# Attention with memory and a two-layer MoE on one core: the keys' and queries' high part, and the memory matrix's low part, move to GpSimd

## The chip, the cores and the metric

One core of a Trainium2 chip runs the kernel. The metric is the device time of one execution in microseconds. The core has a tensor engine (PE, whose weight loads are PEld), VectorE (DVE), ScalarE (ACT), GpSimd (POOL), and SyncE (SP), on whose queue nearly all DMAs of this kernel are issued.

## The reference

Four batches with eight heads of 576 positions and 64 features go through causal attention plus a read of a memory matrix; the result of all heads is one row of 512 features per position and goes through two dense layers with a gate between.

```python
def _attn_ref(q, k, v, M_prev, z_prev, beta):          # q, k, v: (4, 8, 576, 64)
    scores = scale * np.matmul(q, k.transpose(0, 1, 3, 2))
    scores = np.where(causal, -1000000000.0, scores)
    a = np.exp(scores - scores.max(-1, keepdims=True))
    a /= a.sum(-1, keepdims=True) + 1e-09
    local = np.matmul(a, v)
    q_p = phi(q)                                        # x > 0 ? x + 1 : exp(x)
    mem_out = (q_p @ M_prev) / (q_p @ z_prev + 1e-06)   # per head
    g = 1.0 / (1.0 + np.exp(-beta))[None, :, None, None]
    return g * mem_out + (1 - g) * local

def _moe_ref(x, w_in, w_out):                           # x: (2304, 512)
    h = x @ w_in                                        # w_in: (512, 2048)
    g = h * (1.0 / (1.0 + np.exp(-1.702 * h)))
    return g @ w_out
```

## The kernel before, in words

Matrix products run on PE in a rounded 32-bit type (F32R). To keep precision an operand is split into a high part, which is the operand rounded to F32R, and a low part, the operand less its high part; a product is then made of high times high, low times high and high times low.

Two heads form a pair, so there are 16 pairs: batch b = 0 to 3, pair c = 0 to 3 in it. For every pair `load_kq` and `load_vq` (L343 to L365) load keys and queries into `kqr` (128 partitions, 576 + 640 columns), values into `vr`, the memory matrices into `mr`, queries by rows into `qr` and the normaliser into `zb`. `plan_prep` then prepares them: `split_hi` (L375) makes `hi`, the high part of `kqr`, 1216 columns wide; `split_lo_k` and `split_lo_q` make the low parts `lok` (576 columns) and `loq` (640) on POOL; `stack_hi` and `stack_lo` copy the three by DMA into the operand `W`; `vhi` and `vlo` split the values into `vs`; `msplit` (L418) makes `ms`, the memory matrix times the head's gate `gt`, in a high and a low part; `qmin`, `qexp`, `qphi` (L438) make `qp`, phi of the queries, which is then divided by its norm. Pairs of batch 0 go another way for `ms` (`mplain`) and compute fewer columns, since part of that batch is done at the start; the other 12 pairs use `msplit`. `plan_attend` makes the scores `ps` on PE, their mask and maximum on DVE (L499), the exponentials `a` on ACT (L505), their scaling on POOL (L508), the transposes `pt` on PE, their split into two `e` on ACT and DVE, the sums `po` over `vs` and `ms` on PE, and `xf` from `po` on DVE. The last 64 columns of the pair's positions (`at`, `tail`) go a like way. `xstore` (L654) writes `xf` of the pair to the tensor `xd` in HBM.

Once a batch's four pairs are stored, `plan_x` loads its chunks (of 256 and 320 columns for batch 0, of 288 for the others) back as `xl` and splits them into `xh` and `xl`, ACT and POOL. `first_moe` then has filler for PE: 16 blocks of 12 matmuls `pm` per chunk. Each block's result goes as `hk` to a tensor `gd` in HBM. The second layer (`acc`) runs after all attention.

A plan of slots puts the instructions into one program order: an entry of the plan has a slot and a priority, pair p starts at slot `K0[p]`, and a block of filler goes into each slot while there is any. The tile framework then reorders the instructions of every engine by a simulated schedule of its own; so an edit in one place changes the order in many. Each engine works its own list strictly in order, and so does SP's queue. `kqr`, `vr`, `mr`, `qr`, `zb`, `hi`, `lok` and `loq` have one buffer each, `W`, `vs` and `ms` have two: the next pair's load or write waits for the last reader of the one before.

`copy(engine, out, in, scale)` and `sub(engine, out, a, b)` are helpers (L97 and L112), with "A" for ACT, "P" for POOL and "V" for DVE; in the profile they stand as L100 (copy on ACT) and L110 (two-input operations).

Of the kernel before, what the change touches and what calls it, by code (L numbers as in the profile page):

```python
# [12 lines left out]
ALU = mybir.AluOpType  # L13
AX = mybir.AxisListType

B, H, S, D = 4, 8, 576, 64
# [6 lines left out]
SQ = 640  # L23
# [6 lines left out]
def f32(ap):  # L30
    return ap.bitcast(F32)
# [3 lines left out]
def tile_attention_memory_moe(ctx, tc, kq, vq, mem, zz, beta, w_in, w_out, out):  # L35
    nc = tc.nc
# [60 lines left out]
    def copy(eng, dst, src, scale=None):  # L97
        if eng == "A":
            kw = {} if scale is None else {"scale": scale}
            nc.scalar.activation(out=dst, in_=src, func=AF.Copy, **kw)  # L100
        elif eng == "V":
            if scale is None:
                nc.vector.tensor_copy(dst, src)
            else:
                nc.vector.tensor_scalar(out=dst, in0=src, scalar1=scale, scalar2=None, op0=ALU.mult)
        else:
            nc.gpsimd.tensor_copy(dst, src)

    def tt(eng, dst, a, b, op):
        (nc.vector if eng == "V" else nc.gpsimd).tensor_tensor(out=dst, in0=a, in1=b, op=op)  # L110

    def sub(eng, dst, src, hi):  # L112
        tt(eng, dst, src, f32(hi), ALU.subtract)
# [7 lines left out]
        out=mask[:, 384:512], in_=mask[:, 384:512], compare_op=ALU.is_ge, fill=NEG,  # L121
# [4 lines left out]
    for r in range(2):  # L126
        v = maskt[64 * r:64 * r + 64, CH - 64:CH]
        nc.gpsimd.affine_select(
            out=v, in_=v, compare_op=ALU.is_ge, fill=NEG, base=0, pattern=[[-1, 64]], channel_multiplier=1)
# [5 lines left out]
    gt = cst.tile([128, NP], F32, name="gt")  # L135
# [200 lines left out]
    raws = {}  # L336
# [30 lines left out]
    def plan_prep(p):  # L367
        b, c = pairs[p]
        s0 = K0[p] - 8
        P = prep[p] = {}  # L370
        rest = b < MB
        T0 = 2 if rest else 0
        qo = 256 if rest else 0

        def split_hi():  # L375
            kqr = raws[p]["kq"]
            P["hi"] = att.tile([128, S + SQ], F32R, name="hi")
            copy("A", P["hi"][:, :S + SQ - qo], kqr[:, :S + SQ - qo])

        def split_lo_k():  # L380
            P["lok"] = att.tile([128, S], F32R, name="lok")
# [35 lines left out]

        def msplit():  # L418
            P["ms"] = att.tile([128, 2, 2, D], F32R, name="ms", bufs=2)
            copy("A", P["ms"][:, :, 0], raws[p]["m"], gt[:, c:c + 1])  # L420
            nc.vector.scalar_tensor_tensor(
                out=P["ms"][:, :, 1], in0=raws[p]["m"], scalar=gt[:, c:c + 1], in1=f32(P["ms"][:, :, 0]),
                op0=ALU.mult, op1=ALU.subtract)

        qm = qmt[:, T0:, :, :D]

# [35 lines left out]
        def qev():  # L462
# [6 lines left out]
            for pt, a, n in ((P["pt"][0][:, qo:], qo, 512 - qo), (P["pt"][1], 512, 64)):  # L469
                copy("A", qh[:, a:a + n], pt[:, :n])  # L470
                sub("V", ql[:, a:a + n], pt[:, :n], qh[:, a:a + n])

        at(s0 + 1, 50, split_hi)
        at(s0 + 3, 50, split_lo_k)
        at(s0 + 3, 51, split_lo_q)
        at(s0 + 3, 52, stack_hi)
        at(s0 + 4, 52, stack_lo)
        if rest:
            at(s0 + 7, 51, mplain)
        else:  # L480
            at(s0 + 6, 55, vhi)
            at(s0 + 7, 50, vlo)
            at(s0 + 7, 51, msplit)
# [429 lines left out]
```

## Time and profile before

| | |
|---|---|
| time, median of 3 runs (lowest, highest) | 684.53 us (683.67, 687.51) |
| the profiled execution's own time | 687.52 us |
| its span in the trace | 685.6 us |
| busy PE / DVE / ACT / POOL | 629.7 / 435.1 / 396.4 / 263.7 us |

The span runs from the first to the last instruction of the trace. A row of the trace gives an instruction's start in the span and how long it took, then engine, line, operation and its tiles, output first. In brackets stands how long its engine was idle before it and what ended that wait. Matmuls are pipelined, so the times of neighbours overlap.

### The profile page before, as it was taken

How to read it: one execution, taken by the hardware profiler on the slowest of the kernel's cores; microseconds unless marked ns; L12 is line 12 of the kernel's file. 1: busy time of each engine (PE TensorE's matmuls, PEld its weight loads, DVE VectorE, ACT ScalarE, POOL GpSimd, SP SyncE). 2: the span in 40 equal slices, each digit the busy share in tenths (PEclk: the TensorE clock that was granted, in tenths of full speed). 3: DMA queues.
4: the chain of work that ended last, by engine and by line, in shares of the span. 5: the costliest groups of instructions: out<-in, count | busy, mean ns of one | idle time of the engine just before them, and what ended most of it. 6: DMA issues, size and time to landing. Idle time of an engine off the chain costs nothing.

```text
span 685.6 us, 12438 instructions
## 1 busy us (share of the span) xinstructions
PE 629.7 (92%) x3984; PEld 572.3 (83%) x3984; DVE 435.1 (63%) x1112; ACT 396.4 (58%) x960; POOL 263.7 (38%) x303
## 2 busy tenths in 40 slices
PE   4578898799987799999899997999999999999997
PEld 3468686689986699999899997999888888888897
DVE  4987765776758776677657634816865555555453
ACT  5676546787757775777576533614555445454453
POOL 3647545976636793566475202502400000000000
PEclk8699999999999999999999999999999999999999
DMA  8859758888557765766772128936444335344231
GB/s 252 270 158 262 217 139 239 231 211 222 150 156 206 206 186 168 216 164 181 236 206 71 44 79 292 323 115 222 152 123 142 109 102 154 94 126 133 68 125 55
DMA packets 71425, 116.70 MB, mean 170 GB/s; under 512 B 8768, under 2 KB 41024, under 8 KB 71360
## 3 DMA queue, kind: packets, MB, share of 16 engines
q1 hardware_dynamic: 71360, 115.91, 57.8%
q8 instruction: 32, 0.52, 0.3%
q14 instruction: 33, 0.27, 0.1%
HBM read 63.97 MB, written 27.79 MB: 134 GB/s over the span
## 4 chain that ended last, share of the span: by engine, by line
PE 73%; DMA 10%; DVE 7%; ACT 5%; issue 3%; SPq 1%; POOL 1%; ACTq 0%; DVEq 0%; POOLq 0%
PE acc L91 29%; PE pm L91 24%; PE po L91 9%; PE pt L95 6%; PE ps L91 5%; DMA gd<-hk 2%; DMA qr<-in_vq_dram 2%; DMA xl<-xd 2%; DMA xd<-xf 1%; DVE ps L499 1%; DMA fq<-in_vq_dram 1%; DVE ws L180 1%; DVE wr L182 1%; DVE ws L179 1%; DMA mr<-in_mem_dram 1%
## 5 line engine op out<-in xcount | busy, mean ns | idle before, releaser
L91 PE MATMUL pm<-xh,wi 128*128 128x288 f32 (+2 forms) x1024 | 221.3, 305 | 12.3 <-ACT hk L100 6.0
L91 PEld LDWEIGHTS pm<-xh,wi 128*128 128x128 f32 x1024 | 168.0, 192 | 15.9 <-ACT hk L100 6.9
L91 PE MATMUL acc<-gh,wo 128*128 128x512 f32 (+1 forms) x640 | 179.2, 368 | 0.0
L91 PE MATMUL pm<-xl,wi 128*128 128x288 f32 (+2 forms) x512 | 153.6, 301 | 0.1
L91 PEld LDWEIGHTS acc<-gh,wo 128*128 128x128 f32 x640 | 115.1, 189 | 20.1
L91 PE MATMUL acc<-gl,wo 128*128 128x512 f32 (+1 forms) x320 | 115.1, 368 | 0.0
L91 PEld LDWEIGHTS pm<-xl,wi 128*128 128x128 f32 x512 | 98.1, 192 | 0.7 <-POOL xl L110 0.3
L508 POOL TENSOR_SCALAR a<-a,sm,g 128x512 f32<-128x512 f32 (+3 forms) x112 | 71.9, 654 | 64.3 <-DVE sm L547 37.1
L499 DVE CUSTOM_DVE_ANT_0 ps<-ps,mask 128x256 f32<-128x256 f32 (+4 forms) x144 | 69.3, 495 | 20.7 <-PE ps L91 15.5
L813 DVE SCALAR_TENSOR_TENSOR gt<-gt,graw 128x512 f32<-128x512 f32 (+1 forms) x80 | 52.3, 654 | 45.5 <-ACT gt L812 45.0
L91 PE MATMUL po<-e,vs 128*128 128x320 f32 (+3 forms) x416 | 76.3, 308 | 4.5 <-ACT e L100 3.7
L505 ACT ACTIVATE a<-ps,nm 128x512 f32<-128x512 f32 (+3 forms) x112 | 60.2, 540 | 31.9 <-DVE nm L499 26.8
L812 ACT ACTIVATE gt<-graw 128x512 f32<-128x512 f32 (+1 forms) x80 | 47.0, 589 | 54.6 <-DVE gl L110 54.6
L110 DVE TENSOR_TENSOR gl<-gt,gh 128x512 fp32r<-128x512 f32 (+1 forms) x80 | 53.2, 665 | 37.2 <-ACT gh L100 34.1
L110 DVE TENSOR_TENSOR e<-pt,e 128x320 fp32r<-128x320 f32 (+1 forms) x120 | 56.4, 486 | 30.9 <-ACT e L100 30.3
L100 ACT ACTIVATE e<-pt 128x320 fp32r<-128x320 f32 (+4 forms) x136 | 55.7, 435 | 28.0 <-PE pt L95 15.0
L91 PEld LDWEIGHTS po<-e,vs 128*128 128x128 f32 x416 | 64.1, 192 | 9.2 <-ACT e L100 4.3
L100 ACT ACTIVATE gh<-gt 128x512 fp32r<-128x512 f32 (+1 forms) x80 | 47.0, 588 | 42.2 <-PE acc L91 39.6
L91 PEld LDWEIGHTS acc<-gl,wo 128*128 128x128 f32 x320 | 59.4, 189 | 9.9
L91 PE MATMUL ps<-W 128*128 128x512 f32 (+3 forms) x224 | 58.6, 347 | 4.6 <-DVE e L110 2.8
L95 PE MATMUL pt<-ident,a 128*128 128x128 f32 x296 | 57.5, 276 | 0.4 <-ACT a L505 0.4
L100 ACT ACTIVATE hk<-pm 128x288 f32<-128x288 f32 (+2 forms) x64 | 26.2, 409 | 52.5 <-PE pm L91 40.4
(132 smaller groups left out, 962.9 us busy)
## 6 DMA issues: line engine op xcount, KB each, us to landing
graw<-gd SPq DMA_DIRECT2D x64, 256.0 KB, 2.7
gd<-hk SPq DMA_DIRECT2D x96, 144.0 KB, 2.5
wraw<-in_w_in_dram SPq DMA_DIRECT2D x16, 512.0 KB, 4.3
wraw<-in_w_out_dram SPq DMA_DIRECT2D x16, 512.0 KB, 4.6
kqr<-in_kq_dram SPq DMA_DIRECT2D x12, 608.0 KB, 5.3
W<-hi SPq DMA_DIRECT2D x24, 272.0 KB, 3.6
W<-loq SPq DMA_DIRECT2D x48, 128.0 KB, 3.7
W<-lok SPq DMA_DIRECT2D x32, 144.0 KB, 3.3
```

Of the source, the lines that this page charges most:

```text
L91: nc.tensor.matmul(out, l, r, start=start, stop=stop)
L95: nc.tensor.transpose(out, in_, idn)
L100: nc.scalar.activation(out=dst, in_=src, func=AF.Copy, **kw)
L110: (nc.vector if eng == "V" else nc.gpsimd).tensor_tensor(out=dst, in0=a, in1=b, op=op)
L179: nc.vector.tensor_scalar(out=si, in0=si, scalar1=3, scalar2=None, op0=ALU.logical_shift_left)
L180: nc.vector.scalar_tensor_tensor(out=si, in0=raw[:, :, 1], scalar=-2 ** 31, in1=si, op0=ALU.bitwise_and, op1=ALU.bitwise_or)
L182: nc.vector.scalar_tensor_tensor(out=box["r"].bitcast(I32), in0=raw[:, :, 0], scalar=29, in1=si, op0=ALU.logical_shift_right, op1=ALU.bitw ...
L499: nc.vector.tensor_tensor_reduce(out=ps, in0=ps, in1=mk, op0=ALU.add, op1=ALU.min, scale=-0.125, scalar=1e38 if j == 0 else nm[:, j - 1:j] ...
L505: nc.scalar.activation(out=a, in_=ps, func=AF.Exp, scale=-1.0, bias=nm, accum_out=sm)
L508: (nc.vector if eng == "V" else nc.gpsimd).tensor_scalar(out=a, in0=a, scalar1=r, scalar2=gcol, op0=ALU.mult, op1=ALU.mult)
L812: nc.scalar.activation(out=t[:, :n], in_=raw[:, :n], func=AF.Tanh, scale=0.851)
L813: nc.vector.scalar_tensor_tensor(out=t[:, :n], in0=t[:, :n], scalar=1.0, in1=raw[:, :n], op0=ALU.add, op1=ALU.mult)
```

## The change

For pairs of batches 1 to 3, `split_hi`'s copy is made by POOL instead of ACT. For the same pairs `msplit` has another form: ACT first scales `mr` in its own place, then ACT copies it to the high part, and POOL subtracts for the low part; before, ACT scaled into the high part, and one DVE instruction (L421) scaled again and subtracted.

```diff
         def split_hi():
             kqr = raws[p]["kq"]
             P["hi"] = att.tile([128, S + SQ], F32R, name="hi")
-            copy("A", P["hi"][:, :S + SQ - qo], kqr[:, :S + SQ - qo])
+            copy("P" if b else "A", P["hi"][:, :S + SQ - qo], kqr[:, :S + SQ - qo])
...
         def msplit():
             P["ms"] = att.tile([128, 2, 2, D], F32R, name="ms", bufs=2)
-            copy("A", P["ms"][:, :, 0], raws[p]["m"], gt[:, c:c + 1])
-            nc.vector.scalar_tensor_tensor(
-                out=P["ms"][:, :, 1], in0=raws[p]["m"], scalar=gt[:, c:c + 1], in1=f32(P["ms"][:, :, 0]),
-                op0=ALU.mult, op1=ALU.subtract)
+            m = raws[p]["m"]
+            copy("A", m, m, gt[:, c:c + 1])
+            copy("A", P["ms"][:, :, 0], m)
+            sub("P", P["ms"][:, :, 1], m, P["ms"][:, :, 0])
```

The order on the engines is the same up to the preparation of the first pair of batch 1, and differs from there on. On ACT, where that pair is prepared while the last pairs of batch 0 are attended, before:

```order
L100 ACTIVATE ms<-mr,gt 128x128
L100 ACTIVATE xf<-po 64x320
L100 ACTIVATE hi<-kqr 128x1216
L100 ACTIVATE e_1386<-pt 128x320
L431 ACTIVATE qmt<-qr 128x10x64
L505 ACTIVATE a_1417,sum_146<-ps,nm 128x512
```

and changed:

```order
L100 ACTIVATE ms<-mr,gt 128x128
L100 ACTIVATE xf<-po 64x320
L100 ACTIVATE e_1386<-pt 128x320
L431 ACTIVATE qmt<-qr 128x10x64
L100 ACTIVATE mr<-mr,gt 128x128
L505 ACTIVATE a_1417,sum_146<-ps,nm 128x512
```

`hi` no longer stands ahead of the `e`, and the scaling of `mr` stands a little behind it; the copy to `ms` follows some rows later.

On POOL, at the second pair of batch 1 (`vs`, `lok` and `loq` are that pair's, the `a` belong to attention), before:

```order
L110 TENSOR_TENSOR vs<-vr,vs 128x10x64
L110 TENSOR_TENSOR qp<-qp,nrm 128x640
L110 TENSOR_TENSOR lok<-kqr,hi 128x576
L110 TENSOR_TENSOR loq<-kqr,hi 128x640
L508 TENSOR_SCALAR at<-at,st,g1t 128x576
L508 TENSOR_SCALAR a_1608<-a_1608,sm,g_136 128x512
L508 TENSOR_SCALAR a_1632<-a_1632,sm,g_136 128x512
L508 TENSOR_SCALAR a_1665<-a_1665,sm,g_136 128x384
```

and changed:

```order
L508 TENSOR_SCALAR at<-at,st,g1t 128x576
L110 TENSOR_TENSOR vs<-vr,vs 128x10x64
L107 CAST hi<-kqr 128x1216
L110 TENSOR_TENSOR qp<-qp,nrm 128x640
L508 TENSOR_SCALAR a_1609<-a_1609,sm,g_136 128x512
L508 TENSOR_SCALAR a_1633<-a_1633,sm,g_136 128x512
L110 TENSOR_TENSOR ms<-mr,ms 128x2x64
L508 TENSOR_SCALAR a_1666<-a_1666,sm,g_136 128x384
L508 TENSOR_SCALAR a_1685<-a_1685,sm,g_136 128x384
L110 TENSOR_TENSOR lok<-kqr,hi 128x576
L110 TENSOR_TENSOR loq<-kqr,hi 128x640
```

The copy `hi` and the subtraction for `ms` are new in the list, and `lok` and `loq` moved behind the scaling of four `a`.

On PE, where the filler of the third chunk (the first of batch 1, 288 columns) begins, before:

```order
L91 MATMUL po<-e_3301,vs 128x64
L91 MATMUL ps<-W_2952 128x256 x2
L91 MATMUL ps<-W_2953 128x256 x2
L91 MATMUL ps<-W_2952 128x128 x2
L91 MATMUL pm<-xh,wi_429 128x288 x2
L91 MATMUL pm<-xh,wi_440 128x288 x2
L91 MATMUL pm<-xl,wi_429 128x288
L91 MATMUL pm<-xh,wi_429 128x288 x2
L91 MATMUL pm<-xl,wi_440 128x288
L91 MATMUL pm<-xh,wi_440 128x288 x2
L91 MATMUL ps<-W_2953 128x128 x2
```

and changed:

```order
L91 MATMUL po<-e_3306,vs 128x192
L91 MATMUL pm<-xh,wi_429 128x288 x2
L91 MATMUL pm<-xh,wi_440 128x288 x2
L91 MATMUL po<-e_3307,vs 128x192
L91 MATMUL po<-e_3306,vs 128x64
L91 MATMUL po<-e_3307,vs 128x64
L95 MATMUL pt<-ident,qp 128x128 x5
L91 MATMUL ps<-W_2957 128x256 x2
L91 MATMUL ps<-W_2958 128x256 x2
L91 MATMUL ps<-W_2957 128x128 x2
L91 MATMUL po<-qpt_3045,ms 128x256
```

The first filler stands a little earlier among the attention matmuls, and four of it are followed by 38 of attention, where ten were followed by two. Counted over PE's list, the filler of the second chunk (320 columns) begins after 364 attention matmuls before and after 337 changed, its last stands after 593 and 525, and the third chunk's first after 762 and 748. On SP's queue the load of the second chunk's `xl` stands behind the first `W<-hi` of the third pair of batch 1 before; changed it stands ahead of the `W<-lok` of the second.

## Rows read from the trace of the kernel before

**Rows 1.** The page's first part: each engine's busy time, share of the span and instructions.

```profile
PE 629.7 (92%) x3984; PEld 572.3 (83%) x3984; DVE 435.1 (63%) x1112; ACT 396.4 (58%) x960; POOL 263.7 (38%) x303
```

**Rows 2.** Four stretches: busy time (instructions) of PE, PEld, DVE, ACT, POOL; clock; DMA.

```profile
107.00:145.00 38.00, 31.19 (x177) 25.00 (x177) 23.96 (x87) 28.92 (x76) 29.32 (x29) 0.96 0.89 236
...
145.00:204.70 59.70, 57.98 (x428) 56.95 (x427) 43.01 (x137) 40.38 (x114) 35.32 (x39) 1.00 0.66 179
...
204.70:238.40 33.70, 25.22 (x167) 20.38 (x165) 26.82 (x84) 25.86 (x73) 22.39 (x25) 1.00 0.73 197
...
270.00:420.00 150.00, 147.77 (x1134) 146.43 (x1133) 95.16 (x300) 92.43 (x259) 68.74 (x79) 0.99 0.53 153
```

**Rows 3.** The chain that ended last, from 200 to 240: start, length, what.

```profile
210.80 3.56 DMA xd<-xf
...
228.93 4.46 DMA xd<-xf
...
233.40 4.48 DMA xl<-xd
```

**Rows 4.** POOL in order of time, first, fourteenth and last of 17 rows.

```profile
115.73 3.43 POOL L508 TENSOR_SCALAR a<-a,sm,g 128x512 f32<-128x512 f32 x4 [2.05 <-DVE sm L547]
...
137.27 1.41 POOL L110 TENSOR_TENSOR lok<-kqr,hi 128x576 fp32r<-128x576 f32 x1 [0.71 <-ACT hi L100]
...
141.03 0.81 POOL L508 TENSOR_SCALAR at<-at,st,g1t 128x576 f32<-128x576 f32 x1
```

**Rows 5.** Groups by form: count, busy, mean ns, idle before; L421's minimum/median/maximum.

```profile
L100 ACT ACTIVATE hi<-kqr 128x1216 fp32r<-128x1216 f32 x12 | 14.6, 1213 | 4.9 <-DMA mr<-in_mem_dram 2.9 <-DMA qr<-in_vq_dram 1.3 <-PE ps L91 0.7
...
L100 ACT ACTIVATE ms<-mr,gt 128x128 fp32r<-128x128 f32 x12 | 5.0, 419 | 0.0
...
L421 DVE SCALAR_TENSOR_TENSOR ms<-mr,gt,ms 128x128 fp32r<-128x128 f32 x12 | 11.2, 935 | 2.7 <-ACT ms L100 2.6
...
L421 DVE SCALAR_TENSOR_TENSOR ms<-mr,gt,ms x12: 332/795/3137, 116.9 to 372.8; 128x128 fp32r<-128x128 f32 x12
```

**Rows 6.** Groups of POOL by form: count, busy, mean ns, idle before.

```profile
L508 POOL TENSOR_SCALAR a<-a,sm,g 128x128 f32<-128x128 f32 x24 | 10.6, 450 | 1.2 <-DVE sm L547 0.9 <-ACT xb L100 0.3
...
L508 POOL TENSOR_SCALAR at<-at,st,g1t 128x576 f32<-128x576 f32 x16 | 13.4, 840 | 2.2 <-PE pm L91 1.0 <-DVE st L575 0.9 <-ACT wi L100 0.3
...
L110 POOL TENSOR_TENSOR lok<-kqr,hi 128x576 fp32r<-128x576 f32 x16 | 22.9, 1433 | 10.6 <-ACT hi L100 9.5 <-DMA wraw<-in_w_in_dram 1.1
...
L110 POOL TENSOR_TENSOR loq<-kqr,hi 128x640 fp32r<-128x640 f32 x12 | 18.7, 1558 | 0.0
...
L110 POOL TENSOR_TENSOR xl<-xl,xh 128x288 fp32r<-128x288 f32 x24 | 18.6, 809 | 36.3 <-ACT xh L100 36.3
```

**Rows 7.** ACT and PE in order of time around two copies of hi.

```profile
107.73 1.22 ACT L100 ACTIVATE hi<-kqr 128x1216 fp32r<-128x1216 f32 x1 [1.33 <-DMA qr<-in_vq_dram]
...
109.46 0.33 PE L95 MATMUL pt<-ident,at 128*128 128x128 f32 x1 [0.97 <-ACT e L100]
...
135.98 1.22 ACT L100 ACTIVATE hi<-kqr 128x1216 fp32r<-128x1216 f32 x1 [2.88 <-DMA mr<-in_mem_dram]
...
137.57 0.63 PE L91 MATMUL po<-e,vs 128*128 128x320 f32 x1 [3.50 <-ACT e L100]
```

**Rows 8.** DVE, POOL and PE in order of time around one L421.

```profile
249.16 3.14 DVE L421 SCALAR_TENSOR_TENSOR ms<-mr,gt,ms 128x128 fp32r<-128x128 f32 x1
...
250.60 1.55 POOL L110 TENSOR_TENSOR loq<-kqr,hi 128x640 fp32r<-128x640 f32 x1
...
252.81 0.56 PE L91 MATMUL po<-qpt,ms 128*128 128x320 f32 x2 [0.81 <-DVE xf L110]
```

**Rows 9.** L438: its minimum/median/maximum, and one beside POOL's TENSOR_SCALAR.

```profile
L438 DVE SCALAR_TENSOR_TENSOR qp<-qr,qmt x16: 544/825/1186, 23.7 to 362.3; 128x640 f32<-128x640 f32 x12, 128x384 f32<-128x384 f32 x4
...
217.18 0.82 DVE L438 SCALAR_TENSOR_TENSOR qp<-qr,qmt 128x640 f32<-128x640 f32 x1
...
217.41 1.77 POOL L508 TENSOR_SCALAR a<-a,sm,g 128x384 f32<-128x384 f32 x2 [4.04 <-PE po L91]
```

## The prediction

> **What bounds the kernel now.** I read the engines' totals first: TensorE (PE) is busy 629.7 us of the span of 685.6 [rows 1], so only some 56 us can be won anywhere, and only where PE stands still. The table of stretches says where that is. While filler (the first MoE layer's matmuls of a finished chunk) lies between the attention matmuls, PE is full: 57.98 of 59.70 us in 145 to 204.7, and 147.77 of 150 in 270 to 420 [rows 2]. A pair of heads prepared or attended there costs nothing unless it comes so late that the filler runs out. In the two stretches without filler PE is busy 31.19 of 38 us (107 to 145) and 25.22 of 33.7 (204.7 to 238.4) [rows 2]. Those two are where this change can act: pairs before the fourth batch-0 one keep their code, and the last MoE layer has no attention in it. In the second of them no engine is full: DVE 26.82, ACT 25.86, POOL 22.39 of 33.7 us, that is 80, 77 and 66% [rows 2]. The pairs go through at 18.1 us each (the stores of xf of two neighbours start at 210.80 and 228.93 [rows 3]), and the next filler can start only when the store of the batch's last pair and the load of the stored chunk, 4.46 and 4.48 us, are through [rows 3]. So the pair's chain through DVE, ACT, POOL and PE bounds these stretches, no single engine. In the first stretch POOL is nearest to full: 29.32 of 38 us [rows 2], and between 115.73 and 141.84 its rows leave three short waits, the longest 0.71 [rows 4].
>
> **What one pair's change costs on each engine.** Twelve pairs are concerned. ACT loses the copy hi, 1.21 us, keeps its copy to ms and gets the scaling in place, a second operation like it at 0.42 [rows 5]: 0.79 us less per pair. DVE loses L421, 0.94 us in the mean; its shortest is 0.33 and its longest 3.14 [rows 5], so most of what goes is waiting. POOL gets a copy of 128x1216 and a subtraction of 128x128. The trace has neither on POOL. One-input operations there take 0.450 us at 128 columns and 0.840 at 576 [rows 6], 0.87 ns a column, which gives 1.40 for 1216. A copy without arithmetic might come down to ACT's 1.21. Above, two-input operations bound it: lok and loq together are 1216 columns and 1.43 + 1.56 = 2.99 us [rows 6]. I take 1.40, since the copy has one input. The subtraction is on the line through xl, 0.81 at 288, and lok, 1.43 at 576 [rows 6]: 0.46 at 128. Together POOL gets 1.86 us per pair, between 1.7 and 3.5.
>
> **Term A, the first stretch.** Two pairs' preparations lie in it. On ACT the copy hi stands ahead of an e for which PE waits: hi runs at 107.73 and PE waits until 109.46, 0.97 us for e; hi runs again at 135.98, having waited for its load, and PE waits 3.50 until 137.57 [rows 7]. In the changed order e stands there without hi, so the first wait goes: POOL has room at that time. For the second I set the gain against POOL's new work: 3.50 off PE, and two pairs by 1.86, 3.7, onto a queue that was full from 115.73 to 141.84 [rows 4]. That is -0.97 - 3.50 + 3.7 = -0.8 us. If POOL's work is hidden it is -4.5; if only the first wait goes and POOL's work all counts, +2.7.
>
> **Term B, the matmuls that change their cover.** The scheduler answers the change with another order on PE. Counted in it, the filler of the second chunk begins after 337 attention matmuls (364 before), ends after 525 (593), and the third chunk's begins after 748 (762). So 27 attention matmuls leave the first bare stretch, 41 leave the filled one, 54 join the second bare one and 14 are left for the filled one after it. Bare, a matmul costs 38 us / 177 = 0.215 in the first stretch and 33.7 / 167 = 0.20 in the second; filled, 57.98 / 428 = 0.135 [rows 2]. The sum is -27 x 0.215 - 41 x 0.135 + 54 x 0.20 + 14 x 0.135 = -5.8 - 5.5 + 10.8 + 1.9 = +1.4 us: the filler is spent earlier and the second bare stretch grows from 33.7 us to some 44.6, 2.5 pairs. It rests on the load of the second chunk's x coming as early as the order has it. On SP's queue that load stands ahead of a pair's W<-lok where it stood behind the next pair's W<-hi, so it no longer waits for hi; the W<-hi behind it wait for POOL's copy instead.
>
> **Term C, the second bare stretch itself.** Per pair ACT has 0.79 less and DVE 0.94 less, POOL 1.86 more; the shares become about 72, 74 and 77%. Were ACT's relief all on the pair's chain, it is 2.5 x 0.79 = -2.0; were POOL's work, 2.5 x 1.86 = +4.7. With three engines level I take nothing for this, but for one wait that certainly goes: L421 at 249.16 took 3.14 us while POOL did lok and loq up to 252.15, and PE then waited 0.81 for the xf queued behind it on DVE [rows 8]. -0.8 us. The new waits have their queues too: POOL's copy waits for the load of kqr, and the qp and a behind it wait with it; POOL's low part of ms waits for ACT's two operations, and the next load of mr, which waited for DVE, now waits for POOL.
>
> **Term D, thin filler.** After the third chunk starts, the new order places 4 of its matmuls and then 38 of attention; before, some 20 more filler matmuls stood among those. 20 x 0.135 = 2.7 us of cover, of which I count half, +1.35; nothing if attention runs well there, 2.7 if not. All other preparations lie beside full PE (270 to 420) and cost nothing; POOL's added 1.86 would show only if a pair there lost 18 us against the filler.
>
> **Sum.** -0.8 + 1.4 - 0.8 + 1.35 = +1.15 us. The profiled execution took 687.52 us (685.6 of span and 1.9 around it), the median is 684.53. The sum holds against either; set on the median it gives 685.7. A measurement of this kernel tells about 0.5% (3.4 us) from no change, so this is no change.
>
> **Rivals.** *Faster, ACT and DVE are what the bare stretches wait for.* For it: both are busier than POOL in the second one, and PE's waits behind hi and L421 [rows 7, 8] go with them. Against it: POOL is nearly full in the first. It gives A -4.5, B +1.4, C -2.8, D 0: -5.9, 678.6 us. *Slower, POOL becomes the late engine in the second bare stretch.* The copy waits in POOL's in-order queue for a load and for the buffer that PE's last ps of the pair before frees, and what stands behind it (qp, a, at) feeds PE. It decides if POOL's 1.86 ends last in each of the 2.5 pairs: +4.7 on the sum, 690.4 us. With the copy at 2.99 instead of 1.40 it would be 4.0 more. For it: POOL at 77% in the first stretch, with three waits in 26 us [rows 4]. Against it: 66% in the second. *Slower, POOL's copy holds up DVE.* L421 shows that DVE with two inputs from SBUF can stand still for as long as POOL reads [rows 8]; L438 has two such inputs as well and remains. If POOL's copy stops it for 1.40 in each of 2.5 pairs, that is +3.5, 689.2. Against it: L438 took 0.82 at 217.18 while a one-input POOL operation ran from 217.41, and of its 16 none took over 1.19 [rows 9]; only the two-input operations of POOL stopped DVE there.
>
> The Trainium skill, SBUF — State Buffer, section Who interferes with whom, has a rule on this: a DVE instruction with two SBUF inputs contends with any GpSimd instruction that reads SBUF, and whoever issues first holds the shared ports while the other fully blocks. By that rule the one-input copy would hold L438 as lok and loq held L421, which is the third rival's time; the trace agrees for two-input POOL work (3.14 us against 0.33) and has no row where a one-input one did it.
>
> That the change doesn't do what it says is out: the order has the copy and the subtraction on POOL.
>
> **Chances.** No change 0.39 (681.1 to 688.0), faster 0.29, slower by POOL's queue 0.24, slower by DVE held 0.08. 678.6 and 690.4 are the rivals' times; the bounds of the copy add 4.0 above, and not all of the bare-stretch effects need come together. I take 678 to 693, which leaves out about a tenth on each side.
>
> **What would show it.** In the profile after: hi on POOL at about 1.40; none of hi on ACT, whose sum falls by about 9.5 us, and no L421; PE full to about 190 instead of 204.7, and the next bare stretch some 10 us longer; the 3.50 wait at 137 smaller. Pairs there quicker than 18.1 us speak for the first rival, POOL's share above 85% with PE or ACT waiting for POOL for the second, L438 over 1.5 us for the third. The prediction is wrong if the load of the second chunk does not come earlier, since then B is lost altogether.

## The result, and the profile after

The changed kernel takes 692.57 us (median of 4 runs, 691.6 to 694.65), the kernel before 684.1; the ratio is 1.0121, 95% interval 1.0076 to 1.0165. It is slower by 1.2%, some 8.5 us. The forecast was no change, 685.7, with 681.1 to 688.0 for that case; the time lies outside of these, but in the whole range that was given, 0.4 us below its upper end, and nearest to the 690.4 of the rival on POOL's queue. Ratios and their intervals, here and below, compare executions in the faster of two states alone; one execution of kernel e6 below and two of e8 were in the slower one, so the medians of these two lie above what their ratios say.

The profiled execution took 693.12 us, its span is 691.3. First the page's totals (busy time, share of the span, instructions), to be held against [rows 1]:

```profile
PE 634.5 (92%) x3984; PEld 575.4 (83%) x3984; DVE 426.3 (62%) x1100; ACT 387.0 (56%) x960; POOL 284.7 (41%) x327
```

ACT has 9.4 us less (396.4 before), DVE 8.8 less (435.1), POOL 21.0 more (263.7), and PE, with the same 3984 matmuls, 4.8 more. So the work moved as it was meant to, and PE, which bounds the kernel, stands still no less: 56.8 us of the span here, 55.9 before. The groups of the moved operations, by form (count, then busy time, mean ns, idle before), answer to [rows 5] and [rows 6]:

```profile
L107 POOL CAST hi<-kqr 128x1216 fp32r<-128x1216 f32 x12 | 14.4, 1201 | 11.8 <-DMA gd<-hk 4.3 <-DMA kqr<-in_kq_dram 2.7 <-PE ps L91 2.6
...
L110 POOL TENSOR_TENSOR ms<-mr,ms 128x128 fp32r<-128x128 f32 x12 | 5.5, 459 | 3.0 <-ACT ms L100 1.9 <-PE pt L95 0.9
...
L100 ACT ACTIVATE mr<-mr,gt 128x128 f32<-128x128 f32 x12 | 4.8, 401 | 9.8 <-DMA mr<-in_mem_dram 9.4
...
L100 ACT ACTIVATE ms<-mr 128x128 fp32r<-128x128 f32 x12 | 3.7, 309 | 3.0 <-PE po L91 3.0
```

hi takes 1.20 us on POOL, as long as on ACT (1.21) and less than the 1.40 that the sum used; the subtraction takes 0.46, as worked out.

To see where the time goes, both traces are cut at the same points of the first layer's filler: the last matmul of the first chunk, the first and last of the second, the first and the 64th of the third, and the last of all. The table of stretches (busy time and instructions of PE, PEld, DVE, ACT, POOL, then clock and DMA), before:

```profile
96.80:145.10 48.30, 41.29 (x235) 33.02 (x233) 28.03 (x102) 32.81 (x89) 34.84 (x36) 0.96 0.88 232
...
145.10:204.10 59.00, 57.28 (x423) 56.25 (x422) 42.57 (x135) 39.70 (x111) 34.62 (x38) 1.00 0.67 181
...
204.10:238.40 34.30, 25.82 (x171) 20.97 (x170) 27.18 (x85) 26.43 (x75) 22.99 (x26) 1.00 0.72 194
...
238.40:256.60 18.20, 17.27 (x115) 16.53 (x116) 13.54 (x40) 14.05 (x40) 17.62 (x20) 0.91 0.69 200
...
256.60:484.30 227.70, 221.29 (x1677) 219.18 (x1676) 141.91 (x385) 126.16 (x332) 92.55 (x101) 0.99 0.59 179
```

and the changed kernel:

```profile
99.50:141.80 42.30, 36.25 (x207) 28.56 (x206) 23.70 (x84) 24.97 (x74) 32.32 (x35) 1.00 0.83 218
...
141.80:196.80 55.00, 54.10 (x380) 52.46 (x380) 34.95 (x112) 35.02 (x100) 35.20 (x39) 0.97 0.62 173
...
196.80:241.50 44.70, 35.49 (x227) 30.28 (x225) 33.47 (x113) 31.83 (x94) 33.98 (x38) 0.92 0.69 186
...
241.50:263.10 21.60, 19.18 (x129) 18.07 (x130) 13.75 (x45) 15.65 (x46) 16.75 (x21) 0.92 0.83 203
...
263.10:489.90 226.80, 219.56 (x1676) 216.18 (x1675) 136.87 (x379) 122.72 (x332) 105.09 (x114) 1.00 0.62 183
```

| stretch | before | changed | difference | by the prediction's terms |
|---|---|---|---|---|
| up to the last filler of the first chunk | 96.8 | 99.5 | +2.7 | 0 |
| first bare stretch | 48.3 | 42.3 | -6.0 | -6.6 (A, and 27 matmuls of B) |
| filler of the second chunk | 59.0 | 55.0 | -4.0 | -5.5 (41 matmuls of B) |
| second bare stretch | 34.3 | 44.7 | +10.4 | +10.8 (54 of B) |
| 64 filler matmuls of the third chunk | 18.2 | 21.6 | +3.4 | +2.45 (14 of B, C and D) |
| the rest of the first layer | 227.7 | 226.8 | -0.9 | 0 |

Term C is the wait of PE that ended at 252.81 us [rows 8]. It stands here in the row of the third chunk's filler, where that time lies, though the prediction counts it with the second bare stretch. The 2.7 us of the first row arise where the lists of both kernels are the same; that point lies anywhere from 95.2 to 99.5 us in the traces of this document. Behind it the changed kernel is 2.9 us longer, and the second bare stretch is what makes it so. PE stands still for 9.2 of its 44.7 us, and for 8.5 of 34.3 before; so the stretch is longer by the matmuls that joined it (227 instead of 171 in the rows above), not by longer waits. These two traces thus show 2.9 us of the 8.5. Part of the rest is which execution was traced: that of before took 687.52, 3.4 over its median, that of the changed one 693.12, 0.6 over its own. The granted clock is not what made the changed one slower: over the whole traced execution it is 0.983, and 0.974 before, though the second bare stretch has 0.92 where before has 1.00.

### The profile page after: what moved, and what is told of

It reads as the page before. It is cut to its first block, busy times and chain, and to the rows that moved or that the text cites. A ratio compares the mean times of both kernels' runs of the same rounds, so it can differ in the third digit from the quotient of the medians.

```text
span 691.3 us, 12415 instructions
## 1 busy us (share of the span) xinstructions
PE 634.5 (92%) x3984; PEld 575.4 (83%) x3984; DVE 426.3 (62%) x1100; ACT 387.0 (56%) x960; POOL 284.7 (41%) x327
## 4 chain that ended last, share of the span: by engine, by line
PE 69%; DMA 12%; DVE 7%; ACT 5%; issue 4%; SPq 3%; POOL 1%; ACTq 0%; DVEq 0%; POOLq 0%
PE acc L91 29%; PE pm L91 23%; PE po L91 7%; PE pt L95 5%; PE ps L91 5%; DMA qr<-in_vq_dram 3%; DMA xl<-xd 3%; DMA gd<-hk 2%; DVE ps L499 1%; DMA W<-lok 1%; ACT a L505 1%; DMA mr<-in_mem_dram 1%; DMA fq<-in_vq_dram 1%; SPq L404 1%; DMA wraw<-in_w_in_dram 1%
## 5 line engine op out<-in xcount | busy, mean ns | idle before, releaser
L91 PE MATMUL po<-e,vs 128*128 128x320 f32 (+3 forms) x416 | 78.6, 309 | 0.3 <-ACT e L100 0.2
L505 ACT ACTIVATE a<-ps,nm 128x512 f32<-128x512 f32 (+3 forms) x112 | 60.4, 542 | 32.6 <-DVE nm L499 28.9
L100 ACT ACTIVATE e<-pt 128x320 fp32r<-128x320 f32 (+4 forms) x136 | 54.1, 435 | 31.2 <-PE pt L95 19.3
L91 PE MATMUL ps<-W 128*128 128x512 f32 (+3 forms) x224 | 61.4, 358 | 10.2 <-DMA W<-lok 3.5
L103 DVE COPY hk<-pm 128x288 f32<-128x288 f32 (+2 forms) x64 | 29.0, 453 | 46.2 <-PE pm L91 34.2
```

The costliest lines, as they stand in the source:

```text
L91: nc.tensor.matmul(out, l, r, start=start, stop=stop)
L505: nc.scalar.activation(out=a, in_=ps, func=AF.Exp, scale=-1.0, bias=nm, accum_out=sm)
```

## Experiments

Every edit lets the tile framework order the lists of all engines anew. To part the engines' work from the order, most kernels below hold given lists: once the program is written down, each instruction is tied behind the one that stands ahead of it in a list, by order alone, without a wait for it to end. All such kernels have this at the end:

```diff
+    for engine, text in orders.items():
+        here = [i for i in nc.cur_bb.bb.instructions if str(i.engine) == "EngineType." + engine ...]
+        order = []                       # the list, as runs of numbers into `here`
...
+        for a, b in zip(order, order[1:]):
+            tc.add_manual_dep(b, a.name, mybir.DependencyInfo(NoSync, DATA), reason="order")
```

The results, in us (interval of the ratio to before in brackets; "stretches" are those of the table above, from the last filler of the first chunk to the last of all, in the profiled execution):

| kernel | lists | median | ratio | stretches |
|---|---|---|---|---|
| before | own | 684.1 | | 48.3, 59.0, 34.3, 18.2, 227.7 |
| changed | own | 692.6 | 1.0121 [1.0076, 1.0165] | 42.3, 55.0, 44.7, 21.6, 226.8 |
| e1: changed engines, hi ahead of lok, subtraction left to the scheduler | before's | 701.8 | 1.026 [1.022, 1.0301] | 55.0, 61.5, 36.9, 18.7, 229.3 |
| e2: before's engines | changed's | 707.7 | 1.0328 [1.0283, 1.0373] | 46.1, 57.0, 47.5, 24.5, 234.1 |
| e3: hi alone | own | 704.7 | 1.0289 [1.0256, 1.0322] | 45.2, 57.5, 48.5, 25.8, 229.2 |
| e4: ms alone | own | 688.3 | 1.0059 [1.003, 1.0088] | 46.0, 60.5, 35.8, 15.7, 229.3 |
| e6: changed engines, hi ahead of lok, subtraction at L421's place | before's | 695.6 | 1.0152 [1.0088, 1.0215] | 51.2, 62.7, 35.0, 18.7, 228.9 |
| e7: hi alone, ahead of lok | before's | 698.9 | 1.0197 [1.0141, 1.0253] | 49.2, 65.1, 34.9, 18.7, 229.0 |
| e8: ms alone, subtraction at L421's place | before's | 686.3 | 1.0002 [0.9967, 1.0038] | 48.8, 58.9, 34.0, 16.0, 228.6 |
| e9: POOL makes vs's low part twice | before's | 687.8 | 1.0055 [1.0027, 1.0083] | 50.8, 62.5, 32.4, 16.0, 227.3 |
| e10: hi alone, at ACT's place | before's | 685.2 | 1.0001 [0.9972, 1.003] | 49.5, 60.5, 32.6, 15.6, 224.2 |
| e11: whole change, both at the old places | before's | 684.7 | 0.9999 [0.9977, 1.0022] | 51.3, 59.8, 34.6, 15.5, 224.6 |
| e12: changed, preparation pulled up | changed's, edited | 728.4 | 1.064 [1.061, 1.067] | 47.3, 54.9, 57.6, 24.5, 242.6 |

### The engines or the order

My first theory was the order: the new lists spend the filler with fewer attention matmuls beside it, and that alone is the loss. The rival was POOL's added work. Two kernels cross the engines of one version with the lists of the other, two take the halves of the change with lists of their own.

The first has the changed code and the lists of before:

> The changed engines (hi and the low part of ms on POOL, ms scaled in place on ACT) with every engine's list held in the order of the kernel before: hi stands directly ahead of lok on POOL, the two operations on ms stand on ACT where the one stood, the subtraction on POOL is left to the scheduler. Order theory (the loss comes from the new order of the lists, which takes 67 attention matmuls from beside filler into the bare stretch): the time of before, 684 us, within 3. POOL theory (POOL's added 1.86 us a pair ends last in the bare stretches): as slow as the change, 690 to 694, with the stretch after the second chunk's filler, 33.7 us before, some 4 to 5 us longer.

Measured: 701.76 us (700.63 to 707.42). The 67 matmuls of the expectation are about by how many earlier in PE's list the second chunk's filler ends, 525 instead of 593; by the counts 27 leave the bare stretch before the filler and 41 the filler. The second is the other way round, the code of before with the lists of the change:

> The engines of the kernel before with every engine's list held in the order of the changed one (hi, which is not in ACT's changed list, is left to the scheduler there, and so is L421 on DVE). Order theory: the time of the change, 690 to 694 us; the filler of the second chunk ends near 197 instead of 204 and the bare stretch after it grows by some 10 us. POOL theory: the time of before, 684 us, within 3.

Measured: 707.68 us (703.13 to 711.69). Neither result is what a theory had for it: by the order the first would be near 684, by POOL's work the second. Each crossing is worse than either version with lists of its own. But neither is a clean test, since the operations that are in only one of the versions have no place in the other's lists: the scheduler placed the subtraction in the first, hi and L421 in the second. In the first, POOL's rows around the second pair of batch 1 show one reason:

```profile
127.41 1.20 POOL L107 CAST hi<-kqr 128x1216 fp32r<-128x1216 f32 x1
...
132.56 0.46 POOL L110 TENSOR_TENSOR ms<-mr,ms 128x128 fp32r<-128x128 f32 x1 [3.96 <-ACT ms L100]
...
132.97 2.10 POOL L110 TENSOR_TENSOR lok<-kqr,hi 128x576 fp32r<-128x576 f32 x1
```

hi runs at 127.41 (121.5 before, on ACT), and then POOL stands for 3.96 us at the subtraction, which waits for ACT's ms, with lok behind it. Such waits of that subtraction come to 10.7 us in the run. The scheduler chose this place under lists that were held everywhere else, and the changed kernel doesn't have it, so this run doesn't price the change.

The halves, each with the scheduler's order:

```diff
-            copy("A", P["hi"][:, :S + SQ - qo], kqr[:, :S + SQ - qo])
+            copy("P" if b else "A", P["hi"][:, :S + SQ - qo], kqr[:, :S + SQ - qo])
```

> Only the copy hi goes to POOL for batches 1 to 3; msplit as before; the scheduler orders anew. In its order the second chunk's filler lies between attention matmuls 327 and 532 and the third's begins at 751 (before: 364, 593, 762; changed: 337, 525, 748). Order theory: nearly the whole loss, 690 to 694 us. POOL theory: 1.2 of the 1.66 us a pair that POOL got, so 689 to 691.

Measured: 704.72 us (702.8 to 705.52), more than either theory has for it, and 12 us more than with the second half added. The other half, msplit as in the change and hi left on ACT:

> Only msplit is changed (ACT scales in place and copies, POOL subtracts); hi stays on ACT; the scheduler orders anew. The second chunk's filler lies between attention matmuls 350 and 590 and the third's begins at 762, almost as before. Order theory: 683 to 685 us, the L421 waits gone and nothing lost. POOL theory: POOL gets 0.46 us a pair, 685 to 687.

Measured: 688.27 us (685.72 to 693.05), again more than either theory has, and 0.6% over before; the whole interval, 1.003 to 1.0088, is above 1, while the lists are almost those of before. The halves don't add up: +20.6 and +4.2 against +8.5 for both. Which order the scheduler comes to moves the time by more than the whole change does.

### hi's place or the subtraction's

The kernel before was traced a second time:

> The kernel before once more, for a second trace of it: its first one was of an execution of 687.5 us, 3.4 over the median. Both theories: 682 to 686 us, with the end of the first layer's filler some 3 us earlier than 484.3.

This execution took 688.11 us, so it is no trace of a median run either; its stretches, 50.1, 58.0, 34.7, 18.2 and 226.9, repeat those of the first trace within 2 us each. The end of the filler, 485.0, is not earlier than the first trace's, as was expected. The table's picture of before stands, and it is that of executions some 3.4 us over the median.

Then the subtraction was put where L421 ran, in the changed code with the lists of before. POOL's list at the second pair of batch 1:

```diff
 L107 CAST hi<-kqr 128x1216
-L110 TENSOR_TENSOR ms<-mr,ms 128x2x64
 L110 TENSOR_TENSOR lok<-kqr,hi 128x576
 L110 TENSOR_TENSOR loq<-kqr,hi 128x640
 L508 TENSOR_SCALAR at<-at,st,g1t 128x576
 L508 TENSOR_SCALAR a_1609<-a_1609,sm,g_136 128x512
...
 L508 TENSOR_SCALAR a_1666<-a_1666,sm,g_136 128x384
+L110 TENSOR_TENSOR ms<-mr,ms 128x2x64
```

> As the new engines in the old order, but POOL's subtraction for ms stands where L421 ran in the trace of before (behind lok, loq and at of the pair as a rule) instead of where the scheduler put it, ahead of lok, where POOL waited 10.7 us in sum for ACT's ms. Place theory (the 17 us of that run came from this place of the subtraction): 685 to 690 us. hi theory (they came from hi standing in POOL's full in-order list, behind which lok, the loads and W come late): 696 to 701 us.

Measured: 695.62 us (693.23 to 703.86), ratio 1.0152 where the subtraction ahead of lok gave 1.026. The place of the subtraction was some two fifths of that run's loss, so neither theory has it all. The halves in the lists of before part the rest:

> Only hi goes to POOL, directly ahead of lok, and every list is held in the order of the kernel before; msplit as before. hi theory: most of the 17 us, 694 to 700 us, hi of batch 1's second pair 4 us or more later than in before. Place theory: 684 to 688 us.

Measured: 698.92 us (693.38 to 700.48).

> Only msplit is changed, hi stays on ACT, every list is held in the order of the kernel before, and POOL's subtraction stands where L421 ran. hi theory: 682 to 685 us, the waits in L421 gone and nothing else changed. Place theory: the same to 2 us more. If it is over 687 us, the subtraction costs by itself, through the longer hold on mr or POOL's list.

Measured: 686.32 us (679.42 to 689.71), ratio 1.0002. The new msplit costs nothing and gains nothing within 0.4% either way, though L421 and its waits, up to 3.14 us [rows 5], are gone. What costs in the lists of before is hi on POOL, directly ahead of lok.

### POOL's load or hi's place in its list

hi on POOL can cost for two reasons: POOL has 1.2 us more to do per pair, or hi has to wait for its turn where ACT could make it as soon as its load was there. The first was tried without hi, by work that changes nothing:

```diff
         def vlo():
-            sub("P", P["vs"][:, :, :, 1], ...)
+            for again in range(2 if b else 1):
+                sub("P", P["vs"][:, :, :, 1], ...)
```

> The kernel before in its own order, all engines as before, but POOL makes the low part of vs twice in each of the 12 pairs (the same subtraction again right behind itself, 1.56 us; the output stays the same): POOL's load without hi's move. Load theory (POOL's list is so full in the bare stretches that any 1.2 to 1.6 us a pair more comes out at the end): as dear as hi's move or dearer, 694 to 702 us. Place theory of hi (what costs is that hi must now wait for its turn in POOL's in-order list, where ACT could make it as soon as kqr was there, so that W and the next kqr come later): 684 to 688 us.

Measured: 687.79 us (684.62 to 692.97), +3.7, ratio 1.0055 with an interval that excludes 1. The doubled group in its trace:

```profile
L110 POOL TENSOR_TENSOR vs<-vr,vs 128x640 fp32r<-128x640 f32 x24 | 37.5, 1562 | 3.4 <-ACT vs L100 2.4
```

Twelve times 1.56 us more on POOL, more than hi takes there, come out as 3.7 us, not as the 14 of hi. The second reason was tried by moving hi alone within POOL's list, from directly ahead of lok to where ACT ran it in the trace of before. That moves it in eight of the twelve pairs, by up to six entries; nothing else differs between the two kernels:

> Only hi goes to POOL and every list is held in the order of before, as in the run with hi directly ahead of lok, but hi stands earlier in POOL's list: where ACT ran it in the trace of before, up to four scalings of a and qp further ahead of lok. Place theory: it regains much of the 14 us, 685 to 690 us. Load theory: no gain, 695 to 701 us.

Measured: 685.17 us (680.33 to 686.3), ratio 1.0001: the some 14 us of the kernel with hi directly ahead of lok (698.92) are gone. One place in POOL's list, at the third pair of batch 2:

```diff
 L110 TENSOR_TENSOR qmt<-qp,zb 128x10x64
+L107 CAST hi<-kqr 128x1216
 L110 TENSOR_TENSOR qp<-qp,nrm 128x640
 L508 TENSOR_SCALAR a_3075<-a_3075,sm,g_136 128x256
 L508 TENSOR_SCALAR a_3110<-a_3110,sm,g_136 128x256
-L107 CAST hi<-kqr 128x1216
 L110 TENSOR_TENSOR lok<-kqr,hi 128x576
```

POOL and SP's load of kqr in order of time there, in the run with hi ahead of lok:

```profile
227.29 1.55 POOL L110 TENSOR_TENSOR qmt<-qp,zb 128x640 f32<-128x640 f32 x1
...
230.77 1.26 POOL L110 TENSOR_TENSOR qp<-qp,nrm 128x640 f32<-128x640 f32 x1 [1.93 <-DVE sm L547]
...
232.02 1.10 POOL L508 TENSOR_SCALAR a<-a,sm,g 128x256 f32<-128x256 f32 x2
...
233.06 1.20 POOL L107 CAST hi<-kqr 128x1216 fp32r<-128x1216 f32 x1
...
234.34 1.41 POOL L110 TENSOR_TENSOR lok<-kqr,hi 128x576 fp32r<-128x576 f32 x1
...
223.77 0.58 SPq L350 DMA_DIRECT2D kqr<-in_kq_dram  x1
```

and in the run with hi at ACT's place:

```profile
221.68 1.57 POOL L110 TENSOR_TENSOR qmt<-qp,zb 128x640 f32<-128x640 f32 x1
...
224.38 1.20 POOL L107 CAST hi<-kqr 128x1216 fp32r<-128x1216 f32 x1 [1.12 <-PE pt L95]
...
225.53 1.26 POOL L110 TENSOR_TENSOR qp<-qp,nrm 128x640 f32<-128x640 f32 x1
...
227.84 1.43 POOL L110 TENSOR_TENSOR lok<-kqr,hi 128x576 fp32r<-128x576 f32 x1
...
218.32 0.58 SPq L350 DMA_DIRECT2D kqr<-in_kq_dram  x1
```

The load of kqr is issued at 223.77 in the first and at 218.32 in the second, and such a load takes 5.3 and 5.4 us in the median (DMA parts of their pages). So hi could run from about 229.1 in the first; POOL stands there for 1.93 us at qp, which waits for DVE, and hi comes at 233.06, 9.3 us after the issue of its load. In the second it comes 6.1 us after it, in the gap ahead of qp. Behind hi hang its DMAs to W and, since kqr has one buffer, the next pair's load. So an engine that is busy for only two thirds of a stretch can still be a bad home for an operation, if the list has it behind one that waits.

The whole change was then put together in the same way, changed code and lists of before, hi where ACT had it and the subtraction where DVE had L421:

> The whole change (hi and ms's low part on POOL, ms scaled in place) with every list in the order of the kernel before; hi stands in POOL's list where ACT ran it in the trace of before, the subtraction where L421 ran. Place theory: the change costs nothing by itself, 682 to 687 us, against 695.6 with hi directly ahead of lok and 692.6 in the scheduler's own order. Load theory: POOL has 1.66 us a pair more, 690 to 696 us.

Measured: 684.71 us (681.72 to 687.45), ratio 0.9999, interval 0.9977 to 1.0022. Its totals are those of the changed kernel:

```profile
PE 633.3 (92%) x3984; PEld 576.8 (84%) x3984; DVE 425.3 (62%) x1100; ACT 387.9 (57%) x960; POOL 282.7 (41%) x327
```

POOL has 282.7 us here and 284.7 in the changed kernel, ACT 387.9 and 387.0, DVE 425.3 and 426.3, and one takes 684.7 us, the other 692.6. With lists that suit it the moved work is free to within 0.25%, and brings nothing either; the 8.5 us of the change are the order in which its lists stand. So the first theory comes back in its wider form: the changed engines with the order of before take the time of before, as it had forecast for e1, once the moved operations have their old places too. That the matmuls beside the filler are the whole loss is not shown by this. The ties that hold the lists cost nothing that shows: e8, e10 and this kernel have them, and ratios of 0.9999 to 1.0002.

### What in the changed kernel's own lists costs

In the trace of the changed kernel the preparation of the third pair of batch 1 shows what its lists do. POOL's hi and lok, and SP's issues between the load of qr and the first DMA of hi to W:

```profile
148.07 1.20 POOL L107 CAST hi<-kqr 128x1216 fp32r<-128x1216 f32 x1
...
157.27 1.43 POOL L110 TENSOR_TENSOR lok<-kqr,hi 128x576 fp32r<-128x576 f32 x1
...
153.83 1.02 SPq L704 DMA_DIRECT2D gd<-hk  x2
...
155.67 0.84 SPq L362 DMA_DIRECT2D qr<-in_vq_dram  x1
...
156.61 0.47 SPq L395 DMA_DIRECT2D W<-hi  x1
```

hi is done at 149.27, and its DMA to W is issued 7.3 us later, since SP's list has stores of hk and the load of qr ahead of it; lok stands 9.2 us behind hi. In the kernel before, hi ran at 135.98 [rows 7] and its DMA was issued at once:

```profile
137.22 0.47 SPq L395 DMA_DIRECT2D W<-hi  x1
```

This pair lies beside filler, where PE stands for only 0.9 of 55.0 us. In the pair before it, the second, such a delay reaches PE, at the end of the first bare stretch. In the changed kernel's trace the load of the second chunk's xl, W<-lok behind it on SP's queue, and PE's wait, then what W<-lok took from issue to landing over the whole run:

```profile
133.24 0.60 SPq L692 DMA_DIRECT2D xl<-xd  x1
...
133.93 1.22 SPq L401 DMA_DIRECT2D W<-lok  x2
...
141.41 0.64 PE L91 MATMUL ps<-W 128*128 128x512 f32 x1 [3.51 <-DMA W<-lok]
...
DMA to landing us min/median/max: 2.3/3.3/7.4
```

lok began 6.0 us behind hi there (125.56 and 131.52), and its DMA, issued 0.7 us behind the load of xl, landed after 7.4 us, the longest of all; the load itself took 7.8. PE stood 3.51 us for it. So the load that the new order puts ahead of W<-lok, which lets the filler begin earlier, had a wait of PE right behind it. It is one wait of 3.5 us in a stretch that is 6.0 shorter than before, and e11 has one of 2.89 there for something else; it is not shown to be what the kernel loses.

One kernel pulled the chain from hi to W up, on POOL and SP, and left PE, DVE and ACT as the change has them. On SP's list, at this pair:

```diff
-L704 DMA gd_100<-hk 128x320
-L704 DMA gd_101<-hk 128x320
-L362 DMA qr<-in_vq_dram 128x640
 L395 DMA W_1909<-hi 64x1088
 L396 DMA W_1909<-hi 64x512
 L395 DMA W_1910<-hi 64x1088
 L396 DMA W_1910<-hi 64x512
+L401 DMA W_1909<-lok 64x576
...
+L350 DMA kqr<-in_kq_dram 128x1216
+L704 DMA gd_100<-hk 128x320
+L704 DMA gd_101<-hk 128x320
+L362 DMA qr<-in_vq_dram 128x640
```

> The changed kernel with its own lists on PE, DVE and ACT. On POOL lok and loq stand directly behind hi (in the changed list up to nine operations lie between them), and on SP the DMAs W<-hi, W<-lok, W<-loq of a pair and the next load of kqr are pulled up to where the trace of the changed kernel has hi, lok and loq done, ahead of stores of hk and loads that wait for others. Place theory, with the late chain from hi to W as what costs the 8.4 us: 684 to 688 us. If PE's list is what costs (68 attention matmuls fewer beside the second chunk's filler, which this run keeps): 690 to 695 us, as the changed kernel.

Measured: 728.37 us (726.25 to 731.13). Neither number that was expected is near. Its waits, summed by what is waited for (total us, times, longest), on SP and PE from 100 to 430:

```profile
SPq L395 <- POOL hi L107: 29.8, 11, 10.7
...
SPq L362 <- DVE qp L438: 28.2, 7, 9.1
...
PE po L91 <- DVE xf L110: 21.6, 9, 6.1
```

and the same on PE in the changed kernel:

```profile
PE po L91 <- DVE xf L110: 4.6, 4, 2.0
```

SP's queue now stands for 29.8 us at the DMAs of hi that were pulled up, against 6.4 in the changed kernel, and what is queued behind waits with it. One reason is that hi came later than in the trace that the places were read from: the seventh of the twelve at 240.78, in the changed kernel at 231.51. The sum of such waits is no price by itself, since e11 has 15.1 us of them and loses nothing. The edit made waits of its own, and doesn't tell whether the late chain from hi to W is what costs in the changed kernel. Shown is that the loss is the lists' and not the engines' (e11). Which entries of its lists it is stays open. The traces show that the lists take 41 matmuls of attention from beside filler (not the 68 of the expectation) and have 54 more in the second bare stretch. From the first chunk's last filler to the last of all the changed kernel takes 390.4 us; before takes 387.5 and 387.9 in its two traces, and e8, e11 and e10, whose ratios are all within 0.0002 of 1, take 386.3, 385.8 and 382.4. A difference of 2.9 us between two traces is thus within what single traces of equally fast kernels differ by, and only stretches that differ by more, as the second bare one does, can be read from them.

## Why the prediction came out as it did

**What bounds the kernel** was read rightly: the difference arises in the bare stretches and in what filler is left for them, and the second bare stretch grew from 34.3 to 44.7 us, to the 44.6 that was worked out. The load of the second chunk came earlier, as B needs: at 133.24 us instead of 137.78.

**Term A**, the first bare stretch, holds with the part of B there: -6.6 by the sum, -6.0 in the traces. Its two waits of 0.97 and 3.50 us are gone, and in their place stands PE's 3.51 at 141.41 for W<-lok (above). That this is near the 3.7 which was set against them is chance, since that DMA took 4.1 us over its median to land, and no term had this. **Term B**, the matmuls that change their cover, holds stretch by stretch to within 1.5 us in the traces.

**Term C** took nothing for the relief of ACT and DVE against POOL's load, and that holds: e11 has 0.9999 for all the moved work with lists that suit it. The one wait that would "certainly" go did not. L421 went, but PE waits for an xf of DVE at about the same point of the changed kernel, and longer than the 0.81 before:

```profile
246.85 0.50 PE L91 MATMUL po<-qpt,ms 128*128 128x256 f32 x2 [1.96 <-DVE xf L110]
```

It also lies behind the start of the third chunk's filler, not in the second bare stretch as the text has it. **Term D** is +1.35 with bounds of 0 and 2.7. With C and the 14 matmuls of B its stretch should grow by 2.45 and grew by 3.4; without C's gain it would be 3.25.

**What failed is the size of the sum for the order, and the step that set it on the median.** The sum gave +1.15; between the traces, behind the stretch where both lists are the same, it is +2.9; between the medians it is +8.5. The text said that the sum "holds against either", the profiled execution or the median. It does not: all its rates were read from an execution 3.4 us over its median, and a second trace was no better. As e11 shows the rest of the change to be worth nothing, the new order costs all of the 8.5 us, where B and D have 2.75. They price no wait that the new lists make elsewhere, such as the 1.96 us above. Where a usual execution of before is quicker than the two that were traced, no trace shows, so how the 8.5 us are spread over the stretches stays open.

**That the time lies in the range is luck.** Its upper end, 693, is the 690.4 of POOL's load in every bare pair with some room for a copy of 2.99 us; the load costs nothing in e11, and the copy takes 1.20. The forecast itself, no change, did not come true.

**The signs** that were given come out mixed. hi takes 1.20 us, not 1.40; PE is full to 196.8, not 190; ACT's sum fell by 9.4 us, and the bare stretch grew by 10.4, as forecast. Two pairs' stores in the second bare stretch start 16.9 us apart (216.35 and 233.23), quicker than 18.1, which was to speak for the faster rival, while those before them are 20.5 apart. POOL is busy for 33.98 of 44.7 us there, 76% and not 85. The longest L438 is 1.12 us.

**A weak point of the method**: taking each list as given and pricing only what it moves. e2 has the changed kernel's lists, but for the places of hi and L421, and is 15 us slower than it; e3 moves less and is 12 slower. The price of an order depends on how every wait in it falls, and bounds of some microseconds around a sum of moved matmuls are too narrow for that.

**The rivals.** The faster one is out: with L421 gone and nothing else (e8) the ratio is 1.0002, and with all of the relief of ACT and DVE (e11) 0.9999, so the gain that it counted on is not there. The one on POOL's queue named the right place, the in-order list in which hi waits with others behind it, and the time nearest to the result. Its price for load alone, 1.86 us in each of 2.5 pairs, 4.7 us, is about what e9 measured: 1.56 us a pair, +3.7. But the change also takes load off ACT, and load is not what it pays for: e11 has the same load and no loss. So its 690.4 is near by chance. The rival on DVE held by POOL's copy did not come true, as no L438 of the changed kernel ran beside a hi on POOL, but the reason given against it was wrong (below). By the Trainium skill, SBUF — State Buffer, section Who interferes with whom, it had a mechanism, and the traces agree with it: an L438 took 1.19 us where another takes 0.81 (below).

## What to carry to other kernels

When a scheduler orders the lists, an edit is two changes: the work that moves, and a new order of everything behind it. Price them apart: hold the old order, put the moved operations where the old ones ran in the trace, and measure; here that alone showed the work to be free and the order to cost 1.2%. On an engine that works its list in order look at what the moved operation is queued behind, and at the waits of that, before looking at the engine's busy share: some 14 us hung on a place a few entries further up.

## What the runs showed of the hardware

A copy without arithmetic on POOL is as fast as on ACT: 1.201 us for 128x1216 (rows of the changed kernel above) against 1.213 [rows 5]. The line drawn through the scalings of a, 1.40, was too high.

One-input operations of POOL do hold up DVE's L438. The prediction denied it, and said that the trace has no row of it; the trace has one. L438 with POOL idle, and L438 begun while a scaling of a was running, in the trace of before, with that scaling (two instructions, the second from about 236.4 to 237.06):

```profile
265.42 0.81 DVE L438 SCALAR_TENSOR_TENSOR qp<-qr,qmt 128x640 f32<-128x640 f32 x1
...
236.55 1.19 DVE L438 SCALAR_TENSOR_TENSOR qp<-qr,qmt 128x640 f32<-128x640 f32 x1
...
235.76 1.30 POOL L508 TENSOR_SCALAR a<-a,sm,g 128x384 f32<-128x384 f32 x2 [3.22 <-PE pt L95]
```

The first takes 0.81 us, the second 1.19 and ends 0.68 after the scaling. The other way round, in [rows 9], L438 began first at 217.18 and was not held (0.82), and the two scalings beside it took 1.77 us where two take 1.30. And in the changed kernel lok, begun 0.11 us behind an L438, takes 1.98 instead of 1.43:

```profile
131.41 0.82 DVE L438 SCALAR_TENSOR_TENSOR qp<-qr,qmt 128x640 f32<-128x640 f32 x1 [1.27 <-PE pt L95]
...
131.52 1.98 POOL L110 TENSOR_TENSOR lok<-kqr,hi 128x576 fp32r<-128x576 f32 x1
```

In these rows the one that begins first is not held, and the other's time in the trace includes its wait. By the Trainium skill, SBUF — State Buffer, section Who interferes with whom, the one that issues second is blocked until the first is done; these rows agree, with one input on POOL's side as with two. The 1.19 that the prediction took for a bound of L438 is its time behind one scaling.
